# Group 0 of a gated recurrence with a softplus MLP: its chunks in flight, its pass over the weights and its second product, replanned

## The chip, the cores and the metric

One core of a Trainium2 chip runs the kernel. The metric is the device time of one execution in microseconds (us), the median of the runs shown. The core has five engines with a queue each: PE (TensorE, matrix products into PSUM), DVE (VectorE), ACT (ScalarE), POOL (GpSimd) and SP, which here only issues transfers. Each works through its own instructions in the order in which they stand and waits for others by semaphores.

## What is computed

```
# a_re, a_im, q, k, v: 4 batches x 8 heads x 768 steps x 48
mag = sqrt(a_re**2 + a_im**2)
a_re_n, a_im_n = a * min(mag, 0.999) / (mag + 1e-6)
for t in range(768):
    S = a_n[t][:, None] * S + outer(k[t], v[t])     # complex a_n, complex S
    y[t] = q[t] @ S.real
x = y as 3072 tokens x 384
h = x @ w_in                                        # 384 x 2048
out = (max(h, 0) + log1p(exp(-abs(h)))) @ w_out     # 2048 x 384
```

The weights come as 64-bit floats, two 32-bit words each.

## The kernel before

**Tiling.** The 768 steps are cut into 6 groups (g) of 128 steps. A group has 4 chunks, one for each batch, so 24 chunks (gc = 4 g + b). Inside a chunk the recurrence is attention: `pre` (slices: one chunk each in group 0, two chunks each later) makes the logarithm and the angle of the decay, sums both over the 128 steps and turns q and k by them. The sums are, in group 0, products with a triangle of ones on PE (line 548, `sum`, of fp32), later scans on DVE (line 531). The angle needs Arctan and Sin, which ACT has in another table than Ln and Exp, so each visit costs table loads (line 895, `trig`). `chunk` then transposes k (661), moves the turned q and k by transfers into the tile qk (642, 646), makes the 128x128 scores (688), masks them (692), multiplies them and the state s by v and q (721, 724), and adds k x v to the state (749). The result goes to the tiles xt0 and xt1 as a high part and a low rest (732 to 734).

**The two products.** `moe` takes a group's 512 columns (4 chunks of 128 steps) through the 2048 inner columns in 16 blocks f of 128: the first product h of 9 matmuls (line 784), |h|, Exp, Ln, max + add (789 to 792), a split into gh and gl (794 to 796) and the second product into three PSUM banks o of 9 matmuls (808). The 9 are three high and low combinations for each of three parts, in a faster 4-byte format; values and weights are split into a high part and a low rest for it. mm2 of a block stands LAG = 2 blocks behind its mm1.

**The weights.** 8 blocks wi and 8 blocks wo are loaded as raw words (378), put together by DVE (388 to 394, `bits`) and split (401 to 405); the split tile lies where the raw words lay. Group 0's slices use four of these buffers for their own work (t_0 to t_3) before the weights come. Group 0 goes only through the first half of the blocks, then group 1 through all of them, then group 0 through the second half: the list `SEGS`. The half sums of group 0 are stored in memory and read back (the tile park, 822 to 830). Near the end ACT inspects all weights again (`seen`, 430 and 431).

**What sets the order.** Each step is a task with an engine, a duration, keys from the table K and buffers. `Planner.order` plays the program with these durations and writes down, engine by engine, which ready task with the smallest key comes next; the built program has each engine's instructions in that order. Where PE has nothing to do between the first sum and the first second product, the planner puts in a filler: a product of the identity with itself that nobody reads (line 844), so many of them as fit. Their number is fixed in the program: on the chip PE works through all of them.

Of the kernel before, what the change touches and what calls it, by code (L numbers as in the profile page):

```python
# [21 lines left out]
P = 128  # L22
# [22 lines left out]
SEGS = [(0, 0, NF // 2), (1, 0, NF), (0, NF // 2, NF)] + [(g, 0, NF) for g in range(2, NGRP)]  # L45
CSTEP = 0.05

# [46 lines left out]
class Planner:  # L94
    WIN = 3.4133
    FREE = 0.2
    SWITCH = (0.2, 0.1)
# [46 lines left out]
    def order(self, filler, until, gate):  # L144
# [14 lines left out]
        for t in reversed(self.tasks):  # L159
            t.key = min([t.key] + [o.key for o in t.outs])  # L160
# [26 lines left out]
        while done < n:  # L187
# [20 lines left out]
            for e in engines:  # L208
# [25 lines left out]
                if best is None and e == "PE" and ends and gate.end and not until.end:  # L234
                    t = Task("PE", 0.214, filler, 0, -1, None, 0)
# [60 lines left out]
class Prog:  # L296
# [15 lines left out]
    def consts(self):  # L312
# [19 lines left out]
        self.park = dram.tile([DM, GT], F32, tag="park", name="park")  # L332
        self.chk = c.tile([P, self.nchk], F32, tag="chk", name="chk")

    def masks(self):
# [3 lines left out]
        tri = self.tri = Buf(self.p, "lt", [P, GT], F32, "tri", NLT)  # L339
# [19 lines left out]
    def weights(self):  # L359
# [3 lines left out]
        self.w = {}  # L363
        for j in range(2 * NWP):
# [10 lines left out]
            k = K["wgt"][j]  # L375

# [4 lines left out]
            if self.wwords == 1:  # L381
                add("DVE", d2(n), lambda raw=raw, bits=bits, n=n: V.tensor_copy(
                    bits()[:, :n].bitcast(F32), raw().bitcast(F32)), k, r=[raw], w=[bits])
            else:
                def words(raw, i):
# [8 lines left out]
                add("DVE", d1(n), lambda raw=raw, bits=bits, n=n: V.scalar_tensor_tensor(  # L394
                    bits()[:, :n], words(raw, 0), 29, bits()[:, :n], ALU.logical_shift_right, ALU.bitwise_or),
                    k, r=[raw], w=[bits])

            def flat(t, i):
                return t()[:, i].rearrange("p a b -> p (a b)")

            x = add("ACT", a1(n), lambda bits=bits, fin=fin, n=n: A.activation(
                flat(fin, 0), bits()[:, :n].bitcast(F32), AF.Copy), k, r=[bits], w=[(fin, 0)])
            x.alt["DVE"] = (d2(n), lambda bits=bits, fin=fin, n=n: V.tensor_copy(
                flat(fin, 0), bits()[:, :n].bitcast(F32)))
            add("DVE", d1(n), lambda bits=bits, fin=fin, n=n: V.tensor_tensor(
                flat(fin, 1), bits()[:, :n].bitcast(F32), flat(fin, 0).bitcast(F32), ALU.subtract),
                k, r=[bits, (fin, 0)], w=[(fin, 1)])
            self.w[kind, b] = fin

    def inspect(self):  # L410
# [3 lines left out]
        for j in range(4 * NWP):  # L414
# [15 lines left out]
            add("ACT", a1(n), lambda top=top: A.activation(top(), top(), AF.Abs), k, w=[raw])  # L430
            add("ACT", a1(n, 2), lambda top=top, j=j: A.activation(
# [3 lines left out]
    def pre(self, si):  # L435
# [7 lines left out]
        first, last = g == 0, g == NGRP - 1  # L443
        chk = self.chk
# [14 lines left out]
        if first:  # L459
            t = Buf(self.wpool, f"w{'io'[si % 2]}{NWP - 1 - si // 2}", [P, 2 * NI * WCOL], F32R, f"t_{si}")  # L460
            t1, t2, t3 = (((t, j), lambda j=j: t()[:, j * W : (j + 1) * W].bitcast(F32)) for j in range(3))
            t4, t5 = t2, t1
        else:
            t1, t2, t3, t4, t5 = ((z, lambda z=z: z()[:, :W]) for z in
                                  (Buf(p, "t", [P, 2 * NI * CH], F32, f"t{j}_{si}", NT) for j in range(1, 6)))
        (t1, v1), (t2, v2), (t3, v3), (t4, v4), (t5, v5) = t1, t2, t3, t4, t5
# [31 lines left out]
        for c in range(m):  # L498
            gc = g * B + b0 + c
            vt = self.vt[gc] = Buf(p, "vt", [P, VW], F32, f"v{gc}", 2)  # L500
            add("SP", 0.45, lambda vt=vt, gc=gc: nc.sync.dma_start(vt(), self.vpad[:, gc, :VW]),
                K["chunk"][gc] - K["vlead"], w=[vt], nbytes=4 * VW * P)
            if not last:
                vo = self.vo[gc] = Buf(p, "vo", [P, VO], F32, f"vo{gc}", 1)
                add("SP", 0.45, lambda vo=vo, gc=gc: nc.sync.dma_start(vo(), self.vpad[:, gc, VW:]),
                    K["state"][gc] - K["vlead"], w=[vo], nbytes=4 * VO * P)
# [32 lines left out]
        st = m * sc(W // m) + 0.25  # L539

        def sums(j, tag, bufs, src, key):
            ps = Buf(self.ps, tag, [P, 512], F32, f"sum{j}_{si}", bufs)
            v = lambda: ps()[:, :W]

            def mm():
                for i in range(NI):
                    c = slice(i * P, (i + 1) * P)
                    PE.matmul(ps()[:, c], src[1]()[:, c], self.tri()[:, :P], start=True, stop=True)  # L548

            t = add("PE", 0.69, mm, key, r=[src[0], self.tri], w=[ps])  # L550
            return ps, v, t

        def keep(j, ps, v, key):
            c = car[j]
            add("DVE", 0.1, lambda: V.tensor_copy(
                c().rearrange("p (b i) -> p b i", b=2)[:, b0 % 2], n3(v())[:, :, CH - 1]), key, r=[ps], w=[(c, b0 % 2)])

        if first:
            lb, vl, opener = sums(0, "h", 2, (t1, v1), at())
            if si == 0:  # L560
                self.gate = opener
        else:
            lb, vl = t1, v1
            add("DVE", st, lambda: scan(0, v1, v1), at(), r=[car[0]], w=[t1] + ([] if last else [car[0]]))
        add("ACT", a1(W), lambda: A.activation(cc(0), c3(vl()), AF.Exp), at(), r=[lb], w=ca, tab="log")
        add("ACT", a1(W), lambda: A.activation(cc(1), c3(vl()), AF.Exp, scale=-1.0),  # L566
            at(), r=[lb], w=ca, tab="log")
        if first:
            keep(0, lb, vl, at())
# [4 lines left out]
        def sincos():  # L574
            A.activation(v4(), v3(), AF.Sin, scale=TURN)
            A.activation(v3(), v3(), AF.Abs, scale=TURN)
            A.activation(v3(), v3(), AF.Sin, bias=self.hpi, scale=-1.0)  # L577

        def turn():
            if first:  # L580
                ab, va, _ = sums(1, f"o{1 + si % 2}", 1, (t3, v3), at("turn"))
            else:
                ab, va = t4, v4
                add("DVE", st, lambda: scan(1, v4, v3), at("turn"), r=[car[1]], w=[t3, t4] + ([] if last else [car[1]]))
            add("DVE", d1(W) if first else d2(W), lambda: V.tensor_scalar(vn(), va(), 1.0 / TWO_PI, None, ALU.mult),
                at("turn"), r=[ab], w=[t5])
            add("DVE", d1(W), lambda: V.scalar_tensor_tensor(v3(), va(), 1.0 / TWO_PI, vn(), ALU.mult, ALU.subtract),
                at("turn"), r=[ab, t5], w=[t3])
            if first:
                keep(1, ab, va, at("turn"))  # L590
# [17 lines left out]
        return (arctan, a1(W), [t3]), (sincos, 2 * a1(W) + a1(W, 1) + 0.28, [t4, t3]), turn, tail  # L608
# [5 lines left out]
    def chunk(self, si, c):  # L614
# [14 lines left out]
        qk = Buf(p, "qk", [2 * D, H, 2 * CH], F32, f"qk{gc}", 2)  # L629
# [19 lines left out]
        for y in range(2):  # L649
            add("SP", 0.62, lambda y=y: heads(y), at(), r=rs, w=[(qk, y)], nbytes=2 * D * NI * 1024)  # L650
        for y in range(2):
            add("SP", 0.62, lambda y=y: shared(y), at(), r=rs, w=[(qk, 2 + y)], nbytes=2 * D * 1024)

        if not last:
            for j in range(2):
# [17 lines left out]
                add("PE", 0.33, trans, at("state"), r=[q for q in rs if q[1] != (zc, 1 - j)], w=[pst])  # L673
                add("ACT", 0.6, evac, at("state"), r=[pst], w=[(kt, j)])

        am = []
        for j in range(2):
# [18 lines left out]
            add("PE", 0.56, score, at(), r=[qk], w=[psc], mode=1)  # L696
# [8 lines left out]
        y = Buf(ps, "att", [P, 512], F32, f"y{gc}", NATT)  # L705
# [476 lines left out]
```

## Time and profile before

| | us |
|---|---|
| median of 3 runs | 586.63 (585.69 to 586.83) |
| profiled execution | 588.07 |
| its span, first to last instruction | 586.4 |
| PE busy | 565.2 |
| ACT busy | 444.8 |
| DVE busy | 433.3 |

The page gives busy time for each engine, a chain of work followed back from the last instruction, and groups of instructions by line. Engines work side by side, so busy times do not add up; a step shortens the time only if the chain goes through it. A matmul in fp32 shows as two records in the trace, one in the faster format as one. Records of neighbours overlap, so the distance from start to start is what a step takes in a row of its kind. The median is 1.4 us below the profiled execution.

### The profile page before, as it was taken

The numbers are of one execution on the slowest core, as the hardware profiler recorded it, in microseconds if no ns is written. First come the engines' busy times: TensorE is split into PE (matmuls) and PEld (weight loads), VectorE is DVE, ScalarE is ACT, GpSimd is POOL, SyncE is SP. The second block draws the span as 40 slices with busy tenths as digits, with TensorE's granted clock in tenths as the row PEclk, the third lists the DMA queues.
The fourth block names the chain that finished last, engine by engine and source line by source line (L and its number), as shares of the span: only waits on it lengthen the run. The fifth ranks groups of instructions, "written<-read, shape, count | busy, mean of one in ns | idle before, by whom it ended". The sixth has DMA issues, their size and how long they took to land.

```text
span 586.4 us, 14531 instructions
## 1 busy us (share of the span) xinstructions
PE 565.2 (96%) x6168; PEld 466.1 (79%) x6168; DVE 433.3 (74%) x665; ACT 444.8 (76%) x785; POOL 3.8 (1%) x23
## 2 busy tenths in 40 slices
PE   1999999999999999999999999999999999999995
PEld 1999887778888778778888877888888888888883
DVE  7999899899998989779885986988734344243432
ACT  7966597857889596886969789599659953589762
POOL 2000000000000000000000000000000000000000
PEclk9999999999999999999999999999999999999999
DMA  8889944423003527276261545504418202077002
GB/s 329 354 258 278 396 104 153 121 61 144 0 1 90 164 55 217 78 195 181 69 169 61 132 148 143 178 16 110 122 47 253 79 15 87 0 216 216 1 0 59
DMA packets 45128, 77.69 MB, mean 132 GB/s; under 512 B 3840, under 2 KB 29440, under 8 KB 45056
## 3 DMA queue, kind: packets, MB, share of 16 engines
q1 hardware_dynamic: 45056, 76.69, 42.7%
q8 instruction: 50, 0.82, 0.6%
q14 instruction: 22, 0.18, 0.1%
HBM read 52.30 MB, written 5.51 MB: 99 GB/s over the span
## 4 chain that ended last, share of the span: by engine, by line
PE 94%; DMA 1%; ACT 1%; DVE 1%; SPq 1%; issue 1%
PE o L808 35%; PE h L784 34%; PE o L844 7%; PE att L688 5%; PE att L724 4%; PE att L721 3%; PE att L749 3%; PE att L661 2%; PE sum L548 1%; DMA vo<-vpad_dram 1%; SPq L646 1%; DMA x<-dense_dram 1%; SPq L642 0%; ACT lt L789 0%; ACT x L515 0%
## 5 line engine op out<-in xcount | busy, mean ns | idle before, releaser
L784 PE MATMUL h<-xt,wi 128*128 128x512 f32 x864 | 218.6, 398 | 0.0
L808 PE MATMUL o<-gh,wo 128*128 128x512 f32 x576 | 198.1, 400 | 0.0
L784 PEld LDWEIGHTS h<-xt,wi 128*128 128x128 f32 x864 | 160.2, 188 | 37.6 <-issue 1.2
L808 PEld LDWEIGHTS o<-gh,wo 128*128 128x128 f32 x576 | 108.3, 188 | 26.6 <-issue 1.2
L792 DVE SCALAR_TENSOR_TENSOR lt<-h,lt 128x512 f32<-128x512 f32 x96 | 65.9, 687 | 81.7 <-ACT lt L791 81.6
L808 PE MATMUL o<-gl,wo 128*128 128x512 f32 x288 | 113.6, 394 | 0.0
L789 ACT ACTIVATE lt<-h 128x512 f32<-128x512 f32 x96 | 56.9, 594 | 45.2 <-PE h L784 44.4
L796 DVE TENSOR_TENSOR gl<-lt,gh 128x512 fp32r<-128x512 f32 x96 | 66.1, 689 | 18.4 <-ACT gh L795 17.5
L791 ACT ACTIVATE lt<-lt,fixed 128x512 f32<-128x512 f32 x96 | 69.3, 722 | 1.9
L808 PEld LDWEIGHTS o<-gl,wo 128*128 128x128 f32 x288 | 54.3, 189 | 11.6 <-DVE gl L796 0.2
L790 ACT ACTIVATE lt<-lt 128x512 f32<-128x512 f32 x96 | 60.6, 632 | 1.8
L795 ACT ACTIVATE gh<-lt 128x512 fp32r<-128x512 f32 x58 | 36.6, 631 | 31.7 <-DVE lt L792 30.4
L844 PE MATMUL o<-ident 128*128 128x128 f32 x366 | 44.0, 279 | 0.0
L844 PEld LDWEIGHTS o<-ident 128*128 128x128 f32 x366 | 42.4, 194 | 0.6 <-issue 0.4
L531 DVE TENSOR_TENSOR_SCAN t<-hold,t 128x384 f32<-128x384 uint8 x40 | 36.1, 945 | 2.0 <-ACT x L566 1.3
L895 ACT ACT_TABLE_LOAD x28 | 35.9, 1283 | 0.4
L688 PE MATMUL att<-qk 96*32 96x64 f32 (+3 forms) x1536 | 33.7, 235 | 1.2 <-issue 1.2
L688 PEld LDWEIGHTS att<-qk 96*32 96x32 f32 x1536 | 30.2, 110 | 5.8 <-issue 4.3
L692 DVE TENSOR_TENSOR a<-att,mask 128x512 f32<-128x512 f32 x48 | 31.3, 683 | 3.5 <-PE att L688 3.1
L603 DVE TENSOR_TENSOR x<-x,t 128x768 f32<-128x768 f32 x24 | 22.2, 952 | 10.1 <-ACT t L577 10.1
L724 PE MATMUL att<-a,v 128*32 128x128 f32 x768 | 25.5, 273 | 0.0
L570 DVE TENSOR_TENSOR x<-x 128x1536 f32<-128x1536 f32 (+1 forms) x14 | 21.3, 1524 | 1.7 <-ACT x L566 1.6
(89 smaller groups left out, 628.5 us busy)
## 6 DMA issues: line engine op xcount, KB each, us to landing
x<-dense_dram SPq DMA_DIRECT2D x20, 768.0 KB, 5.8
qk<-x SPq DMA_DIRECT2D x48, 288.0 KB, 4.3
raw_wo<-w_out_dram SPq DMA_DIRECT2D x8, 768.0 KB, 8.2
raw_wi<-w_in_dram SPq DMA_DIRECT2D x8, 768.0 KB, 8.5
seen<-w_in_dram SPq DMA_DIRECT2D x16, 384.0 KB, 4.3
seen<-w_out_dram SPq DMA_DIRECT2D x16, 384.0 KB, 3.9
v<-vpad_dram SPq DMA_DIRECT2D x24, 224.0 KB, 2.5
qk<-x SPq DMA_DIRECT2D x48, 96.0 KB, 3.9
```

The source lines that it names most:

```text
L531: V.tensor_tensor_scan(out()[:, s], self.hold, inc()[:, s], 0.0, ALU.mult, ALU.add)
L688: PE.matmul(psc()[QT * u : QT * (u + 1), hh * P + f : (hh + 1) * P], q[:, h, CH + f : CH + f + QT], q[:, h, f:CH], start=True, stop=True)
L724: PE.matmul(o(G), v[:, w : w + 32], am[h // 4]()[:, h % 4, :], start=first and prim and G < 4, stop=not prim)
L784: PE.matmul(h()[:, :n], w()[:, q, i, fs], x()[:, i, :n], start=k == 0, stop=k == 3 * NI - 1)
L789: add("ACT", a1(n) - 0.04, lambda: A.activation(tv(), h(), AF.Abs), k, r=[h], w=[t])
L790: add("ACT", a1(n), lambda: A.activation(tv(), tv(), AF.Exp, scale=-1.0), k, w=[t], tab="log")
L791: add("ACT", a1(n, 1), lambda: A.activation(tv(), tv(), AF.Ln, bias=self.one), k, w=[t], tab="log")
L792: add("DVE", d1(n), lambda: V.scalar_tensor_tensor(tv(), h(), 0.0, tv(), ALU.max, ALU.add), k, r=[h], w=[t])
L795: x.alt["ACT"] = (a1(n), lambda: A.activation(gh(), tv(), AF.Copy))
L796: add("DVE", d1(n), lambda: V.tensor_tensor(gl(), tv(), gh().bitcast(F32), ALU.subtract), k, r=[t, gh], w=[gl])
L808: PE.matmul(acc[m]()[:, :n], w()[:, wq, f % 2, ms], x(), start=f == f0 and q == 0, stop=f == f1 - 1 and q == 2)
L844: self.nc.tensor.matmul(self.acc0[0]()[:, :P], self.ident, x, start=True, stop=True)
```

## The change

**Group 0's slices.** All four slices of group 0 share one Arctan part (`PARTS`), their Sin parts are tasks of their own, one for each chunk, which may stand side by side. The cosine's |angle| is no longer an Abs on ACT: DVE clears the sign bit into a tile of its own (`fold`). `sums` is written for one chunk at a time.

**Chunks in flight.** qk of chunk 2 lies in a free xt buffer, v of chunks 2 and 3 and vo of chunks 1 to 3 lie in free g buffers, y of group 0 lies in the banks o1 and o2. The triangle lies in the buffer of wo5 instead of an lt buffer.

**One pass.** Each group goes through all 16 blocks once; `SEGS`, park and its transfers are gone. In group 0 the second product is done in fp32 as it stands: one matmul for each of the three parts, with the weights put together in place (`raw`) and one tile gf in place of gh and gl (`native`, NAT). After group 0's pass `move` copies each wo block, splits it and writes it back for groups 1 to 5.

**The plan.** The planner's durations for fillers, switches and some steps are other numbers, the keys K are new, and `nudge` moves single tasks.

```diff
-SEGS = [(0, 0, NF // 2), (1, 0, NF), (0, NF // 2, NF)] + [(g, 0, NF) for g in range(2, NGRP)]
+NTM = 1
+PARTS = [(0, 1, 2, 3), ()]
+TRIB = 5
+NAT = {"i": 0, "o": 8}
+FILL = 0.2233
-    SWITCH = (0.2, 0.1)
+    SWITCH = (0.13, 0.095)
-        tri = self.tri = Buf(self.p, "lt", [P, GT], F32, "tri", NLT)
+        tri = self.tri = Buf(self.wpool, f"wo{TRIB}", [P, 2 * NI * WCOL], F32, "tri")
...
+            def move(k, kind=kind, b=b, raw=raw, fin=fin, n=n, split=split, val=val):
+                bits = Buf(self.p, "t", [P, NI * WCOL], I32, f"val{kind}{b}", NT)
+                x = add("ACT", a1(n), lambda: A.activation(bits()[:, :n].bitcast(F32), val().bitcast(F32), AF.Copy),
+                        k, r=[raw], w=[bits])
+                x.alt["DVE"] = (d2(n), lambda: V.tensor_copy(bits()[:, :n].bitcast(F32), val().bitcast(F32)))
+                split(k, bits)
+                self.w[kind, b] = fin
...
-            vt = self.vt[gc] = Buf(p, "vt", [P, VW], F32, f"v{gc}", 2)
+            vt = self.vt[gc] = Buf(p, "g", [P, GT], F32, f"v{gc}", NG) if gc in (2, 3) else Buf(p, "vt", [P, VW], F32, f"v{gc}", 2)
-                vo = self.vo[gc] = Buf(p, "vo", [P, VO], F32, f"vo{gc}", 1)
+                vo = self.vo[gc] = Buf(p, "g", [P, GT], F32, f"vo{gc}", NG) if gc in (1, 2, 3) else Buf(p, "vo", [P, VO], F32, f"vo{gc}", 1)
...
-            A.activation(v4(), v3(), AF.Sin, scale=TURN)
-            A.activation(v3(), v3(), AF.Abs, scale=TURN)
-            A.activation(v3(), v3(), AF.Sin, bias=self.hpi, scale=-1.0)
+            A.activation(v3(), v3(), AF.Sin, scale=TURN)
+            A.activation(v4(), v4(), AF.Sin, bias=self.hpi, scale=-TURN)
+
+        def fold():
+            add("DVE", d2(W), lambda: V.tensor_scalar(
+                v4().bitcast(I32), v3().bitcast(I32), 0x7FFFFFFF, None, ALU.bitwise_and), at("turn"), r=[t3], w=[t4])
...
+        if gc == 2:
+            room = Buf(p, "xt", [P, 2, NI, GT], F32R, f"qk{gc}", 2)
+        else:
+            room = Buf(p, "qk", [2 * D, H, 2 * CH], F32, f"qk{gc}", 2)
...
+            if native("o", f):
+                gf = Buf(p, "g", [P, GT], F32, "gf", NG)
+                add("DVE", d1(n), lambda: V.scalar_tensor_tensor(gf(), h(), 0.0, tv(), ALU.max, ALU.add),
+                    k, r=[h, t], w=[gf])
+                gs[f] = (gf,)
+                return
...
+                    if native("o", f):
+                        v = w()[:, f % 2 * DM + m * P : f % 2 * DM + (m + 1) * P].bitcast(F32)
+                        PE.matmul(acc[m]()[:, :n], v, gt[0](), start=f == 0, stop=f == NF - 1)
+                        continue
...
-            for part in [(0, 1), (2, 3), ()] + [(s,) for s in range(B, NSL)] + [()]:
+            for part in PARTS + [(s,) for s in range(B, NSL)] + [()]:
...
-            for j, (g, f0, f1) in enumerate(SEGS):
-                self.moe(j, f0, f1, self.xt[g], cols[:, :, g * CH : (g + 1) * CH], parked, K["moe"][j], K["step"][j])
+            for g in range(NGRP):
+                self.moe(g, cols[:, :, g * CH : (g + 1) * CH], K["moe"][g], K["step"][g])
+                if g == 0:
+                    self.move()
...
+    "nudge": {
+        26: 212.6, 54: 90.7, 65: 1174.9, 99: -2921.3, 113: 53.5, 115: 1578.6, 121: 520.0, 126: -506.6,
```

How this moves instructions shows at three places. The first is PE at its first real product, before (line 844 is the filler, 724 the last chunk's y in a bank att, 784 the first product h; wi_489 and the like are single buffers):

```order
L844 MATMUL o_173<-ident 128x128 x19
L724 MATMUL att_94<-a_0_920,v_621 32x128 x6
L724 MATMUL att_94<-a_1_926,v_621 32x128 x6
L724 MATMUL att_94<-a_0_920,v_621 32x128 x2
L724 MATMUL att_94<-a_1_926,v_621 32x128 x2
L844 MATMUL o_173<-ident 128x128 x12
L784 MATMUL h<-xt_0_550,wi_489 128x512
```

The same place after the change (908 is the filler, 784 the last chunk's y in the bank o2, 846 the first product, 879 the native second product):

```order
L908 MATMUL o_190<-ident 128x128 x7
L784 MATMUL y_782<-a_0_770,v_405 32x128 x6
L784 MATMUL y_782<-a_1_775,v_405 32x128 x6
L784 MATMUL y_782<-a_0_770,v_405 32x128 x2
L784 MATMUL y_782<-a_1_775,v_405 32x128 x2
L908 MATMUL o_190<-ident 128x128 x7
L846 MATMUL h<-xt_530,wi_629 128x512 x18
L908 MATMUL o_190<-ident 128x128 x7
L846 MATMUL h<-xt_530,wi_767 128x512 x9
L879 MATMUL o_190<-gf,raw_wo_182 128x512
```

The fillers ahead of it are 180 in 11 runs before and 92 in 16 shorter runs after; the last run of 7 stands between the first products. The second place is ACT between the first two table visits of group 0, before (572 is Arctan, 565 and 566 the two Exp of a sum; x_106 and t_116 are buffers of group 0's slices):

```order
L895 ACT_TABLE_LOAD
L572 ACTIVATE t_116<-t_116 128x384
L572 ACTIVATE t_121<-t_121 128x384
L895 ACT_TABLE_LOAD
L516 ACTIVATE x_111<-x_111,fixed 128x384
L515 ACTIVATE x_111,chk<-t_140 128x384
L565 ACTIVATE x_106<-sum_0_160 128x3x128
```

and after (614 is Arctan, 603 Exp; the Sin parts, 617 and 618, follow in three further visits, for chunks 1 and 0, 2, and 3):

```order
L966 ACT_TABLE_LOAD
L614 ACTIVATE t_116<-t_116 128x384
L614 ACTIVATE t_122<-t_122 128x384
L614 ACTIVATE t_130<-t_130 128x384
L614 ACTIVATE t_147<-t_147 128x384
L966 ACT_TABLE_LOAD
L603 ACTIVATE x_105<-sum_1_0_171 128x3x128
L603 ACTIVATE x_105<-sum_0_0_184 128x3x128
```

The Arctan of all four chunks stands in one visit. The third place is SP's queue behind chunk 0's qk (702 and 706 are the qk transfers, 388 a weight load, 532 and 536 v and vo; in brackets the engines and transfers that SP waits for):

```order
L706 DMA qk_306<-x_105 96x1x256 [waits DMAHW0_49]
L388 DMA raw_wo_393<-w_out_dram 128x1536 [waits DMAHW1_49,PE_49,Pool_49]
L532 DMA v_405<-vpad_dram 128x448 [waits DMAHW2_49]
L536 DMA vo_414<-vpad_dram 128x192 [waits DMAHW3_49]
L702 DMA qk_418<-x_105 96x1x768 [waits DMAHW4_49]
```

This raw_wo is wo5, whose buffer held the triangle; it waits for PE, and v and vo of chunk 3 and qk of chunk 1 stand behind it. Before, only a vo stood between the qk of chunks 0 and 1.

## Rows read from the trace of the kernel before

**Rows 1.** The page: busy time by engine, and the chain by engine.

```profile
PE 565.2 (96%) x6168; PEld 466.1 (79%) x6168; DVE 433.3 (74%) x665; ACT 444.8 (76%) x785; POOL 3.8 (1%) x23
...
PE 94%; DMA 1%; ACT 1%; DVE 1%; SPq 1%; issue 1%
```

**Rows 2.** PE's waits: what for, us in total, times, longest.

```profile
PE sum L548 <- DVE t L522: 12.0, 1, 12.0
PE att L688 <- issue: 1.2, 2, 1.0
```

**Rows 3.** Stretches: us, busy PE, PEld, DVE, ACT, POOL; clock, DMA, GB/s.

```profile
100.00:160.00 60.00, 59.52 (x690) 47.77 (x683) 57.36 (x84) 45.10 (x73) 0.00 (x0) 1.00 0.26 80
...
550.00:570.00 20.00, 20.00 (x88) 16.21 (x87) 6.73 (x10) 12.45 (x20) 0.00 (x0) 1.00 0.00 1
```

**Rows 4.** Lines by form: records, busy us, mean ns of one, idle before.

```profile
L844 PE MATMUL o<-ident 128*128 128x128 f32 x366 | 44.0, 279 | 0.0
...
L688 PE MATMUL att<-qk 96*32 96x128 f32 x384 | 32.6, 276 | 0.2 <-issue 0.2
...
L688 PE MATMUL att<-qk 96*32 96x32 f32 x384 | 31.5, 196 | 1.0 <-issue 1.0
...
L431 ACT ACTIVATE seen<-seen,fixed 128x384 f32<-128x384 f32 x32 | 20.5, 640 | 0.0
```

**Rows 5.** PE's timeline in the ramp: start, us, instructions (records).

```profile
29.77 1.50 PE L548 MATMUL sum<-tri,t 128*128 128x128 f32 x12
...
37.62 1.30 PE L688 MATMUL att<-qk 96*32 96x32 f32 x63
...
43.74 1.29 PE L688 MATMUL att<-qk 96*32 96x128 f32 x63
...
54.64 7.76 PE L844 MATMUL o<-ident 128*128 128x128 f32 x68
...
78.47 4.43 PE L784 MATMUL h<-xt,wi 128*128 128x512 f32 x18
```

**Rows 6.** Fillers alone in one stretch: us, busy PE, PEld, POOL; clock, DMA.

```profile
18.00:26.00 8.00, 8.00 (x72) 7.96 (x72) 0.00 (x0) 1.00 1.04 420
```

**Rows 7.** DVE's timeline in the ramp, and its busy time there.

```profile
8.96 0.55 DVE L517 SCALAR_TENSOR_TENSOR t<-x,t 128x384 f32<-128x384 f32 x1
9.42 0.55 DVE L512 TENSOR_TENSOR t<-x,t 128x384 f32<-128x384 f32 x1
...
76.85 0.55 DVE L734 TENSOR_TENSOR xt<-att,xt 128x384 fp32r<-128x384 f32 x1
...
5.40:77.40 72.00, 68.00 (x111) 1.00 0.90 315
```

**Rows 8.** SP's timeline in the ramp.

```profile
28.89 1.37 SPq L642 DMA_DIRECT2D qk<-x  x2
...
45.07 1.23 SPq L642 DMA_DIRECT2D qk<-x  x2
...
55.67 1.09 SPq L505 DMA_DIRECT2D vo<-vpad_dram  x1
```

**Rows 9.** ACT's timeline in the ramp.

```profile
13.27 1.28 ACT L895 ACT_TABLE_LOAD   x1
...
37.34 0.52 ACT L576 ACTIVATE t<-t 128x384 f32<-128x384 f32 x1
37.90 0.62 ACT L577 ACTIVATE t<-t,fixed 128x384 f32<-128x384 f32 x1
```

**Rows 10.** PE's timeline near the end: first products of two blocks in turn.

```profile
557.80 2.25 PE L784 MATMUL h<-xt,wi 128*128 128x512 f32 x9
...
561.99 2.25 PE L784 MATMUL h<-xt,wi 128*128 128x512 f32 x9
```

**Rows 11.** PE's timeline at a change to 32-row products.

```profile
200.00 0.40 PE L808 MATMUL o<-gh,wo 128*128 128x512 f32 x1
200.33 0.31 PE L749 MATMUL att<-v,kt 128*32 128x64 f32 x6
```

More of the change, by code (lines that the diff above doesn't have):

```diff
@@ L403, in weights @@
[L403 to L408, printed above, removed]
+                add("DVE", d1(n), lambda raw=raw, bits=bits, out=val if native else lambda bits=bits, n=n: bits()[:, :n], n=n:
+                    V.scalar_tensor_tensor(out(), words(raw, 0), 29, bits()[:, :n], ALU.logical_shift_right, ALU.bitwise_or),
+                    k, r=[bits if native else raw], w=[raw if native else bits])
@@ L410, in inspect, with move @@
+            self.moves.append((j, move))
+    def move(self):
+        for j, move in self.moves:
+            move(K["low"][j])
     def inspect(self):
@@ L537, in scan, with sums @@
                 V.tensor_copy(chk[:, k : k + n], e)
[L539 to L543, printed above, removed]
+        st = m * sc(W // m) + 0.38
+        def sums(j, c, tag, bufs, src, key):
+            ps = Buf(self.ps, tag, [P, 512], F32, f"sum{j}_{si}_{c}", bufs)
+            h = NI * CH
+            v = lambda: ps()[:, :h]
             def mm():
+                if not first:
+                    PE.matmul(v(), self.ident, car[j]().rearrange("p (b i) -> p b i", b=2)[:, c, :, None].to_broadcast([P, NI, CH]),
+                              start=True, stop=False)
@@ L551, in sums, with keep @@
             return ps, v, t
[L553 to L561, printed above, removed]
+        def keep(j, c, ps, v, key):
+            f = car[j]
+            q = (b0 + c) % 2
+            add("DVE", 0.07, lambda: V.tensor_copy(
+                f().rearrange("p (b i) -> p b i", b=2)[:, q], n3(v())[:, :, CH - 1]), key, r=[ps], w=[(f, q)])
@@ new lines, in pre @@
+        part = lambda z, c: z if first else (z, c)
+        one = lambda v: v.rearrange("p (i t) -> p i t", t=CH)
+        if summed:
+            for c in range(m):
+                lb, vl, opener = sums(0, c, "h" if first else "att", 2 if first else NATT, (part(t1, c), v1), at())
+                if si == 0:
+                    self.gate = opener
+                for k in range(2):
+                    add("ACT", a1(W // m) - 0.05, lambda c=c, k=k, vl=vl: A.activation(
+                        cc(k)[:, c], one(vl()), AF.Exp, scale=-1.0 if k else 1.0),
+                        at(), r=[lb], w=ca if first else [(x, (c, 0))], tab="log")
+                keep(0, c, lb, vl, at())
@@ L562, in pre @@
         else:
-            lb, vl = t1, v1
             add("DVE", st, lambda: scan(0, v1, v1), at(), r=[car[0]], w=[t1] + ([] if last else [car[0]]))
[L565 to L569, printed above, removed]
+            for k in range(2):
+                add("ACT", a1(W), lambda k=k: A.activation(cc(k), c3(v1()), AF.Exp, scale=-1.0 if k else 1.0),
+                    at(), r=[t1], w=ca, tab="log")
```

248 lines of the change are left out of this document (137 added, 111 removed), and 27 rows, old and new, of the table K.

## The prediction

> **What bounds the kernel now.** I read the page first, then PE's waits, the stretches, and the timelines of the first 80 us. PE is busy for 96% of the span and is 94% of the chain that ended last [rows 1]; after the 12.0 us before its first sum, no wait of more than 1.0 us is listed for it [rows 2]. From 100 to 160 us it is busy for 59.52 of 60 us, though DVE is at 57.36; near the end DVE has 6.73 of 20 us and ACT 12.45, and PE all 20 [rows 3]. So what counts is how many PE instructions stand in the order and what each costs; work of DVE or ACT counts only where PE would arrive before its result. But not all of PE's time is work: 44.0 us are products of the identity that nobody reads (line 844, two records each, 366 in all) [rows 4]. They stand ahead of and just behind the first real product at 78.47 us [rows 5] and fill the time in which group 0's attention isn't ready. That is the ramp, and there the change takes hold.
>
> **The fillers.** The order has 183 fillers before and 99 after, 84 fewer; 180 and 92 of them stand ahead of the first real product. In a dense run 72 records start in 8.00 us [rows 6], so one filler is 0.222 us and 84 are 18.7 us. The mean over all, ends of runs included, is 44.0 / 183 = 0.240 us [rows 4], which would make 20.2. I take 18.7, since a run's end comes with the work that follows it.
>
> Can the rest keep up? 88 fewer ahead of the first product put it at 78.47 - 19.6 = 58.9 us, with the later start below at 60.3. DVE was busy for 68.0 of the 72.0 us up to its last step for that product (76.85 us) [rows 7]: 110 instructions, 75.1 us by their means, since neighbours overlap a little. The 82 that stand there after the change come to 51.3 us by the same means, so 51.3 / 75.1 x 68.0 = 46.5 us busy, and with the same 4 us idle are done at about 56. In the transfers, chunk 2's qk was issued only at 45.07 and chunk 3's vo at 55.67 us [rows 8], and the longest filler run, 7.76 us from 54.64, stood ahead of that vo's product [rows 5]; the change gives these buffers of their own. Then chunk 3's sine is next to be late: its visit ended at 38.5 us [rows 9]. ACT has two more table loads of 1.28 us ahead of it and four Abs of 0.52 fewer [rows 9], and starts later by the term below: about 40.5. Two products on DVE (1.9 us), the qk transfers (chunk 0 took 8.7 us from issue at 28.89 to scores at 37.62 [rows 5, 8]) and some 4 us for scores, masks, values and copies make 55. Both are ahead of 60.3, so PE's own order still sets the first product.
>
> **The later start.** Three more 384-wide DVE steps stand ahead of the first sum; neighbours of that kind start 0.47 us apart (8.96 and 9.42) [rows 7]: +1.4 us. The bound below is 0, if the fillers behind it were waiting cover; above it is 2.
>
> **The native second product.** Of group 0, 144 matmuls of 512 columns in high and low halves go, 48 whole fp32 ones come. A first and a second product of one block (18 matmuls) start again after 561.99 - 557.80 = 4.19 us [rows 10], 0.233 each, so 33.5 us go. The trace has no fp32 matmul of 512 columns. The fp32 filler has 128 columns in two records of 0.111 us [rows 6]. What a column adds is in the score rows, fp32 as well: 196 ns at 32 columns, 276 at 128 [rows 4], so 0.833 ns a column. A record of 512 columns is then 0.111 + 384 x 0.000833 = 0.431 us, a matmul 0.862, and 48 are 41.4: +7.9 us. Above: the filler four times, 0.889, +9.2. Below: each record at the speed of the 512-column matmul of now, 0.465 for two, 22.3 us, -11.2. I take 0.862, because the score rows have the type and show the slope; the low end is a rival. [...]
>
> **Switches.** Where PE goes from 128-row work to the attention's 32-row products, some time is lost: the last second product starts at 200.00, the next one of the other kind at 200.33 [rows 11], 0.10 more than 0.233. The order has 110 such changes before, 88 after, equally many (16) ahead of the first product: 22 x 0.10 = -2.2 us. Bounds 0 and -3.
>
> **What costs nothing.** Gone are the storing of group 0's half sums and their reload, gl and gh of group 0 on DVE and ACT, and 14 Abs on ACT; added are 14 folds on DVE and 8 copies of w_out on ACT or DVE. All of it lies beside a PE that is 99% busy [rows 3]; if that cover went, each moved w_out block would cost its copy and split, some 2 us, 16 in all, in group 1. The 32 inspections of ACT move together into group 4's time, some 70 us of PE; their second step alone is 20.5 us [rows 4], and 14 blocks of softplus stand between them. The tail is the same code.
>
> **SP's queue.** The load of wo5 now waits for PE's last sum, since the triangle lies in wo5's buffer. Behind it on SP stand v and vo of chunk 3 and qk of chunk 1. That sum was at 29.77 us [rows 5], now 31.2; qk needs up to 8.7 us and a little for the three ahead of it: 41. PE had chunk 1's scores at 43.74 [rows 5]; it now has 18 fewer fillers ahead of them, and 3 us more of other work and the later start: 44. It costs nothing if that sum isn't 3 us late.
>
> **The sum.** -18.7 + 1.4 + 7.9 - 2.2 = -11.6 us. The profiled execution took 588.07 us (span 586.4), so it would be 576.5; the median of the runs is 1.4 below the profiled one: 586.63 - 11.6 = **575.0 us**.
>
> **Rivals.** (a) Thin cover: behind the first second product there are no fillers, so PE simply waits where ACT, DVE or a transfer is late. DVE's 105 instructions from the first product to wo7's last step are 86.7 us by means, 78.5 busy by the ratio above, 83 with idle time as in the ramp; PE's work there is 144 x 0.233 + 48 x 0.862 + 1.6 of fillers + about 9.5 of attention = 86. Three per cent of slack is little, and the squeezed inspections may hold PE too. With 3 to 8 us of such waits: 578 to 583. For it speaks the count; against it, that before, with DVE at 57.36 of 60 us, PE lost half a microsecond [rows 3].
>
> (b) Slower: the same place, but DVE becomes the bound of the whole pass, since each of the 16 weight blocks has to be put together from words within or before it. The time is back at 586.6 once the pass is 11.6 us longer than PE's work, so once DVE takes 97.6 us for its 78.5 busy ones, idle a fifth of the time; at a quarter (105 us) it is 594. Against it: DVE idled 6% in the ramp and 4% from 100 to 160 [rows 3, 7].
>
> (c) More gain: PE arrives later than its inputs at nearly every place of the ramp. Then the two waits of 1.2 us in sum [rows 2] go, the fillers count at 0.240 and the start costs nothing: 575.0 - 1.2 - 1.5 - 1.4 = 571.
>
> (d) A whole fp32 product takes the low price, 0.465: 575.0 - 19.1 = 556.
>
> (e) The change doesn't do what it says: ACT's order shows one arctangent visit but three sine visits for group 0, and 31 table loads against 29 in all. If chunk 3's sine came 8 us later than above, 3 past PE, the time were 578; the fillers gone would still be gone.
>
> **Chances.** Forecast (573 to 578) 0.57; (a) 0.21, of which 0.03 reach to within 1.2 us of the time before; (c) 0.11; (b) 0.06; (d) 0.02; (e) 0.03. The range leaves out (d), (b) and the far ends of (a) and (c): 570 to 581. A measurement of this kernel can tell about 0.2%, 1.2 us, from no change; slower is (b), 0.06, the same is the end of (a), 0.03, faster the rest, 0.91.
>
> **What would show it.** Right: fillers 22 to 24 us busy; first sum at 13 to 13.5, the first real product at 58 to 61 us; records of the native product 0.43 us apart; no wait of PE over 1 us behind it. Wrong: PE waits for gf, wi or raw_wo between 60 and 150 us (a, b), or for lt or h in the last third (a); native records near 0.23 apart (d); a first product that waits for SP or for t on ACT (e).

## The result, and the profile after

The changed kernel takes 580.71 us (median; 579.64 to 580.92) against 586.73 on the same chip: the ratio is 0.9895 (95% interval 0.9876 to 0.9914), 6.0 us less. The forecast was 575.0 us, 11.6 less, with a range of 570 to 581. The profiled execution took 580.82 us, its span is 579.1: 7.3 us shorter than before.

The page of the changed kernel, busy time by engine and chain by engine, beside [rows 1]:

```profile
PE 551.1 (95%) x5952; PEld 439.9 (76%) x5952; DVE 430.9 (74%) x669; ACT 426.8 (74%) x756; POOL 3.8 (1%) x23
...
PE 82%; ACT 7%; DVE 4%; DMA 3%; issue 2%; SPq 0%; ACTq 0%; DVEq 0%
```

PE has 14.1 us less work, but the span is only 7.3 us shorter. PE's waits tell where half of it stayed (engine, line, waited for: us in total, times, longest), beside [rows 2]:

```profile
PE sum L583 <- DVE t L553: 13.7, 1, 13.7
PE att L810 <- issue: 2.7, 1, 2.7
PE att L748 <- issue: 1.9, 1, 1.9
PE h L846 <- DVE lt L862: 1.2, 2, 0.8
PE att L721 <- DVE x L656: 1.0, 1, 1.0
```

Two of these waits name no releaser ("issue") and are longer than the 1.0 us that [rows 2] has of this kind. They lie in the ramp. PE's timeline there (start, us, instructions; in brackets the idle time before):

```profile
45.72 0.26 PE L810 MATMUL att<-vo,kt 128*32 128x48 f32 x6
45.80 0.22 PE L810 MATMUL att<-v,kt 128*32 128x64 f32 x1
48.71 0.25 PE L810 MATMUL att<-v,kt 128*32 128x64 f32 x3 [2.69 <-issue]
...
50.66 3.13 PE L908 MATMUL o<-ident 128*128 128x128 f32 x16
...
58.51 0.66 PE L748 MATMUL att<-qk 96*32 96x128 f32 x22
61.04 1.01 PE L748 MATMUL att<-qk 96*32 96x32 f32 x42 [1.87 <-issue]
61.98 1.83 PE L908 MATMUL o<-ident 128*128 128x128 f32 x14
...
66.33 4.43 PE L846 MATMUL h<-xt,wi 128*128 128x512 f32 x18
```

Each hole lies inside a run of like products whose neighbours have the same operands, so no result is being waited for there. Behind the first hole 16 filler records take 3.13 us where 14 take 1.83 later: the clock is down. The stretches show it (us, busy PE, PEld, DVE, ACT, POOL; granted clock, share of the DMA engines, GB/s):

```profile
46.00:49.50 3.50, 0.81 (x49) 0.80 (x52) 1.24 (x2) 0.35 (x1) 0.00 (x0) 1.00 1.07 265
49.60:52.90 3.30, 3.30 (x45) 3.12 (x37) 2.74 (x4) 0.82 (x2) 0.00 (x0) 0.50 0.92 234
```

PE is idle for most of the first stretch; in the second its granted clock is 0.50. The first real product is at 66.33 us, where 60.3 was forecast.

**Where the time went.** By milestones, before and after: first sum 11.97 to 13.71 (+1.7); from there to the first real product 66.5 to 52.6 us (-13.9); from there to the end of the last product 500.5 to 505.6 (+5.1); behind it 7.4 to 7.2 (-0.3). Together -7.3.

### The profile page after: what moved, and what is told of

It is laid out like the page before. It is cut to its first block, busy times and chain, and to the rows that moved or that the text cites. A ratio compares the mean times of both kernels' runs of the same rounds, so it can differ in the third digit from the quotient of the medians.

```text
span 579.1 us, 14114 instructions
## 1 busy us (share of the span) xinstructions
PE 551.1 (95%) x5952; PEld 439.9 (76%) x5952; DVE 430.9 (74%) x669; ACT 426.8 (74%) x756; POOL 3.8 (1%) x23
## 4 chain that ended last, share of the span: by engine, by line
PE 82%; ACT 7%; DVE 4%; DMA 3%; issue 2%; SPq 0%; ACTq 0%; DVEq 0%
PE h L846 31%; PE o L882 25%; PE o L879 7%; PE att L748 4%; PE o L908 3%; PE att L810 3%; PE att L781 3%; PE att L784 2%; PE att L721 2%; ACT seen L460 1%; DMA seen<-w_in_dram 1%; DMA x<-dense_dram 1%; ACT lt L852 1%; ACT seen L459 1%; DMA seen<-w_out_dram 1%
## 5 line engine op out<-in xcount | busy, mean ns | idle before, releaser
L882 PE MATMUL o<-gh,wo 128*128 128x512 f32 x480 | 161.3, 397 | 0.0
L882 PEld LDWEIGHTS o<-gh,wo 128*128 128x128 f32 x480 | 90.1, 188 | 21.1 <-issue 0.6
L882 PE MATMUL o<-gl,wo 128*128 128x512 f32 x240 | 94.1, 392 | 0.0
L879 PE MATMUL o<-gf,raw_wo 128*128 128x512 f32 x96 | 43.5, 594 | 0.0
L748 PE MATMUL att<-qk 96*32 96x96 f32 (+3 forms) x1536 | 33.5, 236 | 1.9 <-issue 1.9
L879 PEld LDWEIGHTS o<-gf,raw_wo 128*128 128x128 f32 x96 | 17.9, 190 | 17.7 <-issue 16.3
L908 PE MATMUL o<-ident 128*128 128x128 f32 x198 | 27.6, 293 | 0.0
L908 PEld LDWEIGHTS o<-ident 128*128 128x128 f32 x198 | 25.6, 206 | 0.9 <-issue 0.6
L864 DVE TENSOR_SCALAR gh<-lt 128x512 fp32r<-128x512 f32 x52 | 22.0, 425 | 3.7
L865 ACT ACTIVATE gh<-lt 128x512 fp32r<-128x512 f32 x28 | 17.2, 626 | 8.7 <-DVE lt L862 8.6
```

The costliest lines, as they stand in the source:

```text
L748: PE.matmul(psc()[QT * u : QT * (u + 1), hh * P + f : (hh + 1) * P], q[:, h, CH + f : CH + f + QT], q[:, h, f:CH], start=True, stop=True)
L879: PE.matmul(acc[m]()[:, :n], v, gt[0](), start=f == 0, stop=f == NF - 1)
L882: PE.matmul(acc[m]()[:, :n], w()[:, wq, f % 2, ms], x(), start=f == 0 and q == 0, stop=f == NF - 1 and q == 2)
L908: self.nc.tensor.matmul(self.acc0[0]()[:, :P], self.ident, x, start=True, stop=True)
```

## The experiments

Theory **F**, formed on this trace: PE ran out of instructions. The page lists a DMA queue of kind "instruction" with 48 packets and 0.79 MB, so 16 KB each, here called pieces. From the start of the first packet to that of the 46th (26.83 to 541.53 us) PE has 5728 matmul and 5727 weight-load records, 255 a packet, and some records can be missing from a trace; F takes a piece for 256 of them. The place where one piece ends and the next begins is called a boundary. 261 records, most of them small attention products, took 4.41 us (41.61 to 46.02); fillers, by an estimate from their four records in 0.222 us [rows 6], would make a piece last 14 us. So by F thinning the fillers makes PE need pieces faster, at a time when the transfers fill the DMA engines (0.97 of their time from 46.02 to 59.17 us). Rival **D**: PE waits for data, from a transfer that the profile doesn't name. A third reading was that DVE or ACT is late.

Ratios are to the kernel before, run on the same chip; the other numbers are from the profiled executions. "Holes" are waits of PE without a releaser ahead of the first real product.

| run | ratio (95%) | median, us | first real product, us | holes, us |
|---|---|---|---|---|
| changed kernel | 0.9895 (0.9876 to 0.9914) | 580.71 | 66.33 | 4.6 |
| e1_shift | 0.9904 (0.9875 to 0.9934) | 582.81 | 68.98 | 5.3 |
| e2_wide | 0.9865 (0.9844 to 0.9887) | 579.20 | 61.73 | 2.3 |
| e3_late_wi2 | 0.9829 (0.9808 to 0.9850) | 577.76 | 63.55 | 3.1 |
| e4_quiet | 0.9907 (0.9876 to 0.9937) | 581.36 | 61.73 | 1.8 |
| e5_nofill | 0.9879 (0.9847 to 0.9912) | 580.17 | 63.36 | 5.6 |
| e6_late | 0.9866 (0.9817 to 0.9915) | 578.28 | 61.99 | 1.6 |
| e7_late_wide | 0.9842 (0.9802 to 0.9881) | 578.42 | 65.13 | 3.1 |
| e8_late_wide_half | 0.9784 (0.9748 to 0.9819) | 574.77 | 62.43 | 3.8 |
| e9_before_few | 0.9994 (0.9975 to 1.0013) | 586.22 | 77.23 | 0 |
| e10_short | 0.9923 (0.9894 to 0.9953) | 582.00 | 65.87 | 4.1 |
| e11_late_wide_quarter | 0.9815 (0.9792 to 0.9837) | 575.53 | 59.40 | 1.5 |

The kernel before had a median of 586.9 to 587.8 us beside the experiments. Single executions of several of these kernels lie 3 to 7 us apart. The size of a hole differs too where the order is the same: the changed kernel and e10_short have one ramp, with holes of 2.69 and 1.87 us in the one trace and 2.76 and 1.35 in the other. So a profiled execution need not be the median.

### Moving the boundaries

```diff
+            for _ in range(32):
+                self.filler(self.ident[:, :16])
             for t in plan:
```

> 32 narrow fillers (16 columns) stand ahead of PE's first sum, where PE is idle anyway; all else as in the changed kernel. Theory F (PE's idle 2.69 us at 46.0 us and 1.87 us at 59.2 us are waits for its own instructions, which come in pieces of 16 KB): the holes move in the order by 128 records, out of the key-value products and into the work that starts near 42 to 43 us and near 50 or 56 us; holes together 3 to 6 us, time within 2 us of 580.7. Rival D (PE waits there for a transfer of data that the profile does not name): the holes stay ahead of the same products, 2.7 and 1.9 us, and the time is 580.7.

Stretches that end where a hole begins, first of the changed kernel, then of this run (the numbers in brackets behind the first two busy times are PE's matmul and weight-load records):

```profile
0.00:46.02 46.02, 31.35 (x475) 30.14 (x475) 34.89 (x67) 37.85 (x79) 3.82 (x23) 1.00 0.85 292
46.02:59.17 13.15, 10.46 (x255) 9.73 (x256) 8.60 (x13) 2.18 (x4) 0.00 (x0) 0.87 0.97 290
```

```profile
0.00:44.67 44.67, 41.83 (x475) 40.80 (x476) 32.05 (x63) 36.23 (x74) 3.85 (x23) 1.00 0.81 280
44.67:59.19 14.52, 11.11 (x256) 10.14 (x255) 8.83 (x14) 3.59 (x8) 0.00 (x0) 0.88 1.01 288
59.19:65.93 6.74, 5.53 (x129) 5.04 (x128) 5.43 (x9) 1.22 (x2) 0.00 (x0) 1.00 1.02 410
```

The first hole comes behind 950 records in the one and 951 in the other, though 128 more records now stand ahead of the same work. In the changed kernel the next hole comes 511 records later (twice 256, one record missing). In this run holes begin at 52.94, 59.19 and 65.93 us, behind 256, 255 and 257 records more. The products at which PE stopped at 46.02 us now run without a stop. One hole lies in the middle of fillers, which need nothing but the identity:

```profile
58.48 0.71 PE L908 MATMUL o<-ident 128*128 128x128 f32 x4
60.41 0.83 PE L908 MATMUL o<-ident 128*128 128x128 f32 x6 [1.22 <-issue]
```

That is the end of D, and of a late DVE or ACT as the cause of this hole. The holes make 5.3 us, within F's bounds; the median is 0.1 us outside. The time of this run says little, though: the 32 fillers, which were to fall into idle time, held PE until 15.57 us, so that the first sum started 1.9 us later than in the changed kernel. The place of the holes is what this run shows. The kernel before fits too: its 1.0 us of "issue" in [rows 2] comes at 68.10 us, behind 859 + 860 = 1719 records, three pieces of 256 after 951:

```profile
0.00:68.10 68.10, 55.95 (x859) 54.19 (x860) 60.85 (x103) 52.28 (x101) 3.84 (x23) 1.00 0.91 318
```

### Fewer instructions for the same PE time

```diff
+    def wide(self):
+        x = self.ident[:, None, :].to_broadcast([P, 4, P])
+        self.nc.tensor.matmul(self.acc0[0]().rearrange("p (a b) -> p a b", a=4), self.ident, x, start=True, stop=True)
...
+                    for _ in range(run // 4):
+                        self.wide()
+                    for _ in range(run % 4):
+                        self.filler(self.ident)
```

> Each four neighbouring fillers of 128 columns are one of 512 columns: the same PE time (0.857 against 0.888 us), a quarter of the instructions. F: fewer instructions per microsecond between 41 and 66 us, so the two holes shrink from 4.6 us together to 2 to 3.5, and the first real product comes at 63.5 to 65.5 instead of 66.3; time 578 to 580. D, or a late DVE or ACT: holes as before, time 580 to 581.

The holes shrank to 2.3 us, the clock was 1.00 from the start to 47.47 us, and the first product came at 61.73, ahead of what F gave; the time is within F's bounds. Its interval overlaps that of the changed kernel, so the trace shows a shorter ramp, but a shorter time is not shown. The first hole is one piece earlier: behind 347 + 348 = 695 records at 42.60 us, 256 fewer than 951.

```profile
0.00:42.60 42.60, 27.85 (x347) 20.68 (x348) 32.10 (x63) 36.02 (x74) 3.84 (x23) 1.00 0.84 295
```

### Moving transfers

`moved` takes SP's transfers with the first numbers out and puts them behind the one with the last number; all other queues keep their order. 32 is the load of wi2, 40 the last of chunk 3's qk.

```diff
-            for t in self.plan.order(lambda: self.filler(self.ident), self.opener, self.gate):
+            plan = self.plan.order(lambda: self.filler(self.ident), self.opener, self.gate)
+            plan = self.moved(plan, [([32], 40)])
+            for t in plan:
```

> The load of wi2 (768 KB), issued at 40.0 us, stands behind chunk 3's qk on SP. F: the instruction packet asked for at 41.6 us, which started at 46.05 behind that load, starts by 43.5; the first hole is under 1 us, the clock stays at 1.0 from 48 to 53 us, the first real product is at 61.5 to 63.5, time 576.5 to 579. D: chunk 2's qk is issued 1 us earlier, so the hole shrinks by 1 us at most; 579.5 to 580.7.

One load, issued later, and the first hole went from 2.69 to 0.29 us (45.86 to 46.15, at the same product). The instruction packet shows why. In the changed kernel, DMA queues (packets, MB, share of 16 engines) in 46.0 to 46.2 us, and in 41.6 to 46.0, where no such packet starts:

```profile
q1 hardware_dynamic: 20, 0.06, 107.1%
q8 instruction: 1, 0.02, 39.3%
```

```profile
q1 hardware_dynamic: 423, 1.27, 101.3%
```

In this run, 43.7 to 43.9 us:

```profile
q1 hardware_dynamic: 22, 0.06, 82.7%
q8 instruction: 1, 0.02, 30.0%
```

The boundary before it, some 256 records ahead of the hole, was crossed at 41.6 us in the changed kernel and at 41.5 here. So the packet started 4.4 us behind it there and 2.3 here, and the next instruction ran some 2.4 to 2.7 us behind the packet's start in both (48.71 and 46.15). The other traces agree. At this boundary the packet came 4.1 to 4.7 us late in the changed kernel, e1_shift, e5_nofill and e10_short, where wi2 stands in its old place, and 1.9 to 2.3 us late in e3_late_wi2, e4_quiet and e6_late. And all 26 holes of the table end 2.3 to 2.9 us behind the start of an instruction packet, in the changed kernel at 48.71 behind 46.05 and at 61.04 behind 58.67 us; the one of the kernel before ends at 69.12 behind 66.54. How the load holds the packet back is not shown. The clock stayed up:

```profile
49.60:52.90 3.30, 2.36 (x97) 2.04 (x96) 2.01 (x4) 0.49 (x1) 0.00 (x0) 1.00 0.84 307
```

The second hole stayed at 1.90 us, and a new one of 0.94 stands one piece earlier, since PE now arrives there sooner. The first product is at 63.55, just outside F's bounds, the time within them and outside D's; the interval of its ratio does not touch that of the changed kernel.

Two further orders of SP went on from there, the first to empty the DMA engines further:

```diff
+            plan = self.moved(plan, [([32], 40), ([42, 43, 44, 45, 46, 47], 53)])
```

> As the run before, and the two halves of x4, the first half of x5, and wi3, wi6, wi7 stand behind wo7 on SP, so that some 4.6 MB do not move between 50 and 60 us. F: both holes together under 1.5 us, the first real product at 59.5 to 62; behind it DVE waits for x4 and wi3, which costs 2 to 6 us, so that the whole time says little (575 to 582). D: the second hole stays at 1.9 us; the first real product is not ahead of 64.

Holes of 0.29, 0.39 and 1.07 us and a first product at 61.73, as F said, though the sum is 0.25 over its bound. Behind it PE waits 1.7 us for gf, DVE's part of which stands behind the late x4:

```profile
PE h L846 <- DVE gf L856: 1.7, 1, 1.7
```

The whole time gained nothing. The second order leaves x4 and wi3 where they were:

```diff
+            plan = self.moved(plan, [([32], 40), ([45, 46, 47], 53)])
```

> wi2 behind chunk 3's qk as in the run with the late wi2, and the first half of x5, wi6 and wi7 behind wo7, nothing needed earlier than it lands. F: the holes at the third and fourth piece shrink from 0.94 and 1.90 to 0.4 to 0.9 each; first product at 61.5 to 63; time 1 to 2 us under that run. D or no relation to traffic: as that run.

One hole of 1.62 us is left. The first product is at 61.99, as expected, but the median (578.28) is not below that of e3_late_wi2; the intervals overlap. The profiled execution shows F's holes; the gain in time was not shown.

### What a filler is worth

```diff
+            fills = [t for t in plan if t.idx == -1 and t.eng == "PE"]
+            plan = [t for t in plan if t not in fills[63:]]
```

> The last 36 fillers of the changed kernel (behind 48 us) are left out, nothing else. By the prediction's rule they are worth 36 x 0.222 = 8.0 us, with the 1.4 us that the low clock added 9.4: 571 to 573, first real product at 57 to 59. F: about 680 records from the first hole to the first product still come in pieces of 256 that need 4 to 6.5 us each, so the holes grow to 6 to 9 us, the first product is at 62 to 64, time 577 to 579. Thin cover (DVE or a transfer is what comes next): PE waits with a named releaser, DVE or ACT, over 1 us at a time.

36 fillers fewer, and no time gained that can be told: 580.17 us. The first product came at 63.36, as F said, but the time is past F's bound as well, and the holes, 5.6 us, stayed short of the 6 to 9 that it gave. The other part of the loss has names, as the reading of thin cover had it, though with waits below 1 us. PE's timeline around it:

```profile
61.92 0.85 PE L784 MATMUL y<-a,v 128*32 128x128 f32 x20 [0.50 <-DVE a L752]
63.36 0.79 PE L846 MATMUL h<-xt,wi 128*128 128x512 f32 x1 [0.59 <-ACT xt L793]
64.59 8.97 PE L846 MATMUL h<-xt,wi 128*128 128x512 f32 x26 [0.43 <-DVE xt L794]
```

26 records that take 6.1 us at 0.233 take 8.97. The granted clock in that stretch:

```profile
64.00:70.00 6.00, 5.57 (x14) 4.25 (x14) 5.74 (x8) 4.65 (x8) 0.00 (x0) 0.50 1.03 402
```

So the fillers left out here had covered three things: results that come late (the waits of 0.43 to 0.59 us above), pieces of instructions that come late (holes of 5.6 us for 4.6), and the clock (0.50 from 64 to 70 us, where the changed kernel has 1.00 from 60 to 70). The same in the kernel before:

```diff
+            fills = [t for t in plan if t.idx == -1 and t.eng == "PE"]
+            gone = [t for i, t in enumerate(fills) if i * 84 // 180 != (i + 1) * 84 // 180 and i < 180]
+            plan = [t for t in plan if t not in gone]
```

> The kernel before, with 84 of its 183 fillers left out, spread evenly over those ahead of the first real product; nothing else changes. If a filler costs its time wherever it stands: 84 x 0.222 = 18.7 us less, 568. If the fillers of that kernel are cover for results that come late (DVE at 68 of 72 us there): PE waits 10 to 18 us with DVE, ACT or a transfer as releaser, first product at 72 to 78, 580 to 587. F adds holes of no releaser of 1 to 5 us.

As many fillers fewer as the change takes away, and the time is that of before (0.9994, 0.9975 to 1.0013). PE waits instead, here with releasers:

```profile
PE att L749 <- ACT kt L668: 3.4, 1, 3.4
PE sum L548 <- ACT t L572: 3.2, 1, 3.2
PE att L724 <- DVE a L692: 2.6, 2, 1.7
```

Nor does F's hole of 1 us stand in this ramp; there were other waits in which a piece could come. PE's waits with a releaser make 10.9 us between the first sum and the first product, within the 10 to 18 expected of fillers that are cover. The clock was down as well, to 0.72 from 20 to 30 us and 0.66 from 60 to 70 (1.00 in both in the kernel before), by an estimate from these numbers a loss of 6.2 us. The two make 17.1 of the 18.7 us that the fillers took. So the fillers of the kernel before were not free time. It follows, though no run tests it by itself, that what the change gained in the ramp it gained by making the attention's results come earlier; the filler count only shows by how much the planner thought so.

### The native product at another price

```diff
-                        v = w()[:, f % 2 * DM + m * P : f % 2 * DM + (m + 1) * P].bitcast(F32)
-                        PE.matmul(acc[m]()[:, :n], v, gt[0](), start=f == 0, stop=f == NF - 1)
+                        v = self.w["i", f // 2]()[:, 0, m, f % 2 * P : (f % 2 + 1) * P]
+                        for q in range(3):
+                            PE.matmul(acc[m]()[:, :n], v, gt[0](), start=f == 0 and q == 0,
+                                      stop=f == NF - 1 and q == 2)
```

> The changed kernel, but group 0's second product is nine matmuls of the faster format (0.233 us each) for three whole fp32 ones, with a high part of w_in as its weights and gf rounded to that format; so it leaves the real product of group 0 out, and DVE and ACT have the same work as in the changed kernel. If the term of +7.9 us is PE's own and PE bounds the pass: 7.7 less, 573. If DVE, at 19.8 of 20 us from 80 to 120 us, is next: PE waits for gf or lt over 1 us at a time, and 2 to 6 us are gained: 575 to 579.

From the first real product to the end of the last, in the changed kernel and in this run:

```profile
66.33:571.92 505.59, 503.78 (x5121) 395.17 (x5119) 381.49 (x577) 383.83 (x670) 0.00 (x0) 1.00 0.37 109
```

```profile
65.87:569.44 503.57, 498.18 (x5169) 403.68 (x5167) 381.14 (x577) 383.81 (x670) 0.00 (x0) 1.00 0.37 110
```

PE's work is 5.6 us less (7.7 were expected), but the stretch only 2.0: PE now waits 5.4 us in it for 1.8 before. DVE is as full in the pass as it was in the changed kernel (19.79 of 20 us from 80 to 100 and from 100 to 120 there):

```profile
80.00:100.00 20.00, 19.08 (x81) 14.99 (x81) 19.79 (x30) 14.76 (x24) 0.00 (x0) 1.00 0.00 1
100.00:120.00 20.00, 19.06 (x84) 14.21 (x83) 19.74 (x28) 16.57 (x26) 0.00 (x0) 1.00 0.25 57
```

So some 2 us of less work on PE show as time in the stretch; beyond that, results of other engines are late. That DVE alone sets this is not shown: no single wait for gf or lt is over 1 us, as was expected in that case; the waits have 0.2 to 0.8 us each and several releasers, DVE most often. The time as a whole was not shorter, 582.00 us for the 575 to 579 expected. In the profiled execution what comes behind the last product took 9.9 us for 7.2; the trace shows no instruction in that difference, and it stays open.

### Putting the remedies together

```diff
+            plan = self.moved(plan, [([32], 40), ([45, 46, 47], 53)])
...
+                    for _ in range(run // 4):
+                        self.wide()
```

> The run before with the wide fillers. F: the gains add up in part: first product at 59.5 to 61, holes ahead of it under 1.5 us together, clock at 1.0 throughout; 574.5 to 577. If the two remedies act on one and the same hole only: as the better of them alone.

No sum of the two gains is seen: the median is above F's bounds, the first product at 65.13 is 4 us later than F gave, and the interval overlaps those of the remedies alone. In the profiled execution a hole of 2.7 us stands behind 695 records, at 43.72 us. The packet started 4.5 us behind the boundary before it, though wi2 was late; why is open, since in the next run the boundary stood at the same time (39.2 us) and the packet came after 2.2 us. Then each run of fillers was halved, and cut to a quarter:

```diff
+                    run = (run + 1) // 2
```

> The run before with each run of fillers halved (some 47 of 99 units of 0.222 us gone, 10.4 us). By the rule that a filler costs its time: 10 us less, first product at 50. F: pieces of instructions, then DVE and the transfers, take over: first product at 56 to 59, holes 2 to 6 us, among them such with DVE as releaser; 572 to 576.

```diff
+                    run = (run + 3) // 4
```

> As the run with late loads and wide fillers halved, with each run of fillers cut to a quarter (another 3 to 5 us of PE time gone). F: nothing more is gained, since pieces of instructions, DVE's results and a lower clock after long holes take it: 573 to 578, waits with a releaser grow by 2 to 5 us. If a filler costs its time: 570 to 572.

Halved, the time is 574.77 us, 2.2% below the kernel before and, by intervals that don't touch, below the changed kernel: the lowest median of all, though the intervals of the quarter, e3_late_wi2, e6_late and e7_late_wide reach into its own. The ramp of its profiled execution, which at 578.74 us was the slowest of four, is not the best one (a hole of 2.66 us; first product at 62.43, later than F gave). At a quarter the first product comes at 59.40, and the median at 575.53 is no better: DVE's waits have come in place of the fillers, as expected, beside one hole.

```profile
PE att L721 <- DVE x L654: 2.1, 1, 2.1
PE att L721 <- DVE x L656: 1.7, 1, 1.7
PE att L748 <- issue: 1.5, 1, 1.5
```

## Why the prediction was half right

**What bounds the kernel.** Right: PE sets the time before and after (94% and 82% of the chain that ended last), and the ramp is where the change takes hold.

**The fillers, -18.7.** Here it failed, and with it the forecast. The count was right (99), and no row speaks against their price at full clock. But the way from the first sum to the first real product became 13.9 us shorter, for 19.5 that 88 fewer fillers ahead of it make. Of the 5.7 us lost, 4.3 are waits (5.5 in sum for 1.2), most of them holes without a releaser; about 1.7 are the 3.4 us at half clock behind the first hole; the rest has the other sign. The step that failed is the question whether the rest can keep up: it went through DVE, the transfers and ACT and found each early. They were, but for 0.95 us in which PE waited for x on DVE; DVE's own waits of over 1 us in the ramp are for PE or for what ACT made of PE's results. What it didn't ask is whether PE's own instructions keep up. The one sign of it, 1.0 us of "issue" in [rows 2], was booked in rival (c) as time that would go.

**The later start, +1.4.** It measured 1.7.

**The native second product, +7.9.** Right. One block's two products, then the next:

```profile
74.25 2.74 PE L879 MATMUL o<-gf,raw_wo 128*128 128x512 f32 x6
76.42 2.65 PE L846 MATMUL h<-xt,wi 128*128 128x512 f32 x9
78.91 2.74 PE L879 MATMUL o<-gf,raw_wo 128*128 128x512 f32 x6
```

The turn is 78.91 - 74.25 = 4.66 us for 4.19 before [rows 10], 0.47 more, 7.6 over 16 blocks; an fp32 matmul is (4.66 - 4.19 / 2) / 3 = 0.855, for 0.862 forecast. The slope of the score rows carried. Rival (d) is out: it gave 0.465 to a whole fp32 matmul, and here a single record takes nearly that, as the six of a block start 0.43 us apart, and a matmul has two.

**Switches, -2.2.** The 110 and 88 count the changes in both directions, which the prediction's sentence doesn't say; 11 pairs go. The way back costs as much:

```profile
202.45 1.33 PE L748 MATMUL att<-qk 96*32 96x128 f32 x64
203.71 0.51 PE L882 MATMUL o<-gh,wo 128*128 128x512 f32 x1
204.06 0.39 PE L882 MATMUL o<-gl,wo 128*128 128x512 f32 x1
```

0.35 from start to start is 0.12 over 0.233, for 0.10 the other way [rows 11]: 11 x 0.22 = 2.4.

**Behind the first product.** Forecast were 7.9 - 2.2 and four more fillers there, 0.9: +6.6. Measured: +5.1. With the native product at 7.6 and the switches at 2.4 the sum is 6.1; the missing 1.0 us is not traced to rows.

**What costs nothing.** Right: no wait of over 1 us behind the first product, PE busy for 503.78 of 505.59 us. SP's queue behind wo5 cost nothing that the profile names.

**Rivals.** (a) did not come: PE's waits behind the first product and up to the last are 0.2 to 0.8 us. But e10_short shows that it was near, at some 2 us. (b) did not come either, for the same reason, nor (c), which wanted more gain. (e): three sine visits, as its order said, and no wait of PE over 1 us for them. The time lies where (a) lay, for a reason that no rival had. That it is inside the range, by 0.3 us, is luck: the range reached that far for (a).

**What would show it.** Native records at 0.43 us and no wait over 1 us: right. Fillers 27.6 us busy for 22 to 24, the first sum at 13.71 for 13 to 13.5, the first product at 66.33 for 58 to 61: wrong, and the last is the miss.

## What to carry to other kernels

Idle work on an engine that set the time was worth its duration here only as far as what stood behind it came earlier: 84 fillers fewer in the kernel before gave 0.9994 of its time. PE's own instructions were among what had to come: with a large load queued ahead, a stretch of many short matmuls ended in a hole of 2.69 us, and that load issued some microseconds later left 0.29 of it and gave back 3 to 4 us. A wait that names no releaser is worth looking up by record counts: here such holes stood multiples of 256 records apart, give or take one, whatever the work, and each ended 2.3 to 2.9 us behind the start of an instruction packet, which speaks for code that came late. Few large fillers left smaller holes here than many small ones (2.3 us for 4.6), though the gain in time was not clear of the noise. What filler work covers (results, code, the clock) is found by taking some out and looking at what waits then.

## What was not expected of the hardware

PE's instructions came in packets of 16 KB, one for 255 matmul and weight-load records in the mean of 45 packets of the changed kernel; in its ramp a packet started up to 4.4 us behind the boundary before it, and PE went on 2.7 and 2.4 us after the packet's start. With the DMA engines at 1.01 of their time (41.61 to 46.02 us), 261 records in 4.41 us didn't cover this, and PE had a hole of 2.69 us.

PE's granted clock was down behind holes of 2.4 to 2.9 us: 0.50 in the changed kernel from 49.6 to 52.9 us, where the hole of 2.69 ended at 48.71; 0.60 in e5_nofill from 49 to 52 us, behind one of 2.9; and 0.88 in e1_shift in the whole stretch from 44.67 to 59.19 us, which begins with one of 2.39. It was 1.00 across a hole of 1.87 us in the changed kernel (59.17 to 66.33 us) and one of 1.90 in e3_late_wi2 (53.0 to 63.5). It was also down behind several waits in a row: in e5_nofill 0.90 from 60 to 64 us and 0.50 from 64 to 70, behind 0.7, 2.5, 0.5 and 0.6 us within 8 us, so that the first real products ran at 0.50, and in e8_late_wide_half 0.94 from 10 to 40 us, with waits of 1.1 and 1.9 us there. These are cases; no rule is drawn from them.

A whole fp32 matmul of 512 columns took 0.855 us beside 0.233 for one of the faster format, close to four times as long (3.7).
